# Part B of a two-part attention kernel: PSUM copies assigned to ScalarE or VectorE by place, the first K turn ahead of Q's and in two banks, and the output row in another tile's memory

## The chip, the cores and the metric

The kernel runs on one core of a Trainium2 chip. The metric is the device time in microseconds (us) of one execution. The kernel before takes 1997.98 us (median of three runs, 1996.13 to 2001.91).

## The reference

Two attention layers read their own inputs, and their outputs are laid side by side. Part A is a sliding, dilated attention; nothing in it changes here. Part B is a recurrent attention with a memory:

```python
H, Dh = 32, 192; M, seg = 8, 32          # x: (1, 2048, 640)
mem = mem0                               # 8 tokens
for s in range(64):
    xs = x[:, 32*s:32*s+32]
    h = concat([mem, xs])                # 40 tokens
    q, k, v = h @ Wq, h @ Wk, h @ Wv     # 640 -> 32 heads x 192, each
    p = softmax(mask(q @ k.T * Dh**-0.5))
    o = (p @ v) @ Wo                     # 6144 -> 640
    mem = o[:, :8]                       # the next segment needs it
    outs.append(o[:, 8:])
```

The 64 segments of 32 tokens follow one another: the first 8 rows of a segment's output are the memory of the next.

## The kernel before

Part A runs first (some 180 us) and loads part B's weights as it goes. Part B is the loop over 64 calls of `segment(s)`.

**Tiling.** The 32 heads are four groups `g` of eight. `HX` holds the tokens of a segment, turned, in two halves: `main(s)` is the 8 memory tokens and 24 tokens of x, and `ahead(s)` holds the last 8 tokens of x of four segments, which don't depend on the memory and so can be projected in advance, for several segments at once. `project32` (L440) projects 32 tokens for one group of q, k or v: 20 matmuls (5 chunks of the 640 inputs by 4 column tiles) into one PSUM tile `acc`. Each segment projects `main` for all of q, k and v; the `ahead` half is projected again only where `RENEW` says (for K of group r and V of group r+2 in a segment with s mod 4 = r), and for Q of one group at the end of each segment. A renewed projection has 40 matmuls in place of 20.

**Path of Q and K.** `to_sb` (L453) copies `acc` to SBUF (`sb`). `turn` (L458) turns it with three matmuls against the identity, into one PSUM tile `pt` (tag `x`, four buffers). `fill` (L467) copies `pt` to where the scores read it: one copy for Q (`QT`), three for K (`KT`: the outer chunks, and the middle chunk's two halves). `turn_late` (L476) does the same for the `ahead` half and keeps the rows of later segments in `Lb` tiles, from which GpSimd fills `QT` and `KT` when their segment comes.

**Scores, softmax, output.** `scores(g)` (L511) is 16 matmuls. `softmax` (L522) is six instructions on the tile `t1`, which has one buffer: L524, L528, L529 on VectorE, the exponential L530 on ScalarE, L532 and L533 on VectorE. `put_p` (L536) multiplies into `P`. `turn_p` (L545) turns `P` and copies it to `PT`; `mix` (L560) multiplies with V (`Vst`, `LV`) and copies into `OT`, four copies; `project_out` (L574) multiplies `OT` with Wo and adds up over all groups in the PSUM tile `Y`. At the end `Y` is copied to `row`, which is a tile of the tag `t1`; `memory_rows` (L586) turns its first 8 tokens into the next `HX`, and GpSimd's queue sends the other 32 to HBM (L655).

**Who copies.** Nearly all copies out of PSUM go through one function, and so appear under its line, L428:

```python
def evacuate(dst, src):
    copies["n"] += 1
    (nc.scalar.copy if copies["n"] % 2 else nc.vector.tensor_copy)(dst, src)
```

So a copy's engine depends on how many copies came before it.

**Order.** The order of TensorE's work is the order of the code in `segment` (`manual_schedule` for PE). The order on VectorE, ScalarE and GpSimd is the scheduler's. Each engine runs its instructions in order, and waits on the others where data or a buffer asks for it. An instruction that waits holds up all that stands behind it on its engine.

**Weights.** A part of Wq, Wk, Wv and Wo stays in SBUF. The rest (10 units of Wo, 8 of Wk, 6 of Wv, 320 or 384 KB each) is streamed from HBM in every segment through six buffers (`get_unit`, L394), issued from SyncE's queue as a buffer comes free.

Of the kernel before, what the change touches and what calls it, by code (L numbers as in the profile page):

```python
# [7 lines left out]
FP32 = mybir.dt.float32  # L8
BF16 = mybir.dt.bfloat16
# [255 lines left out]
def next_start(m, g, s):  # L265

    for t in range(s + 1, s + 5):
        if (m == "q" and t % 4 == g) or f"{m}{g}" in RENEW[t % 4]:
            return t


def part_b(ctx, tc, B_x, B_mem0, B_Wq, B_Wk, B_Wv, B_Wo, out, ident, n_seg, pre, nbuf, mid):
    nc = tc.nc
    Dm, H, Dh, M, SEG, L = 640, 32, 192, 8, 32, 40
# [92 lines left out]
    def pool(name, **kw):  # L367
        return ctx.enter_context(tc.tile_pool(name=name, reuse_waits="tile", **kw))
# [37 lines left out]
    QT = cpool.tile([128, 12 * L + PADW], BF16, name="QT")  # L406
    KT = cpool.tile([128, 4, 4, L], BF16, name="KT")
# [3 lines left out]
    OT = cpool.tile([128, 12 * L + PADW], BF16, name="OT")  # L411
    free = [cpool.tile([128, 3, 4, M], BF16, name=f"Lb{i}") for i in range(BLOCKS)]
    late = {}
    VW = 448
    LV = [cpool.tile([128, VW], BF16, name=f"Lv{g}") for g in range(GROUPS)]
    Vst = cpool.tile([128, VW], BF16, name="Vst")
# [5 lines left out]
        nc.gpsimd.memset(t[:, 192:256], 0.0)  # L422

    copies = {"n": 0}

    def evacuate(dst, src):
        copies["n"] += 1
        (nc.scalar.copy if copies["n"] % 2 else nc.vector.tensor_copy)(dst, src)  # L428

    def load_x(s):  # L430
        if s < n_seg:
            nc.sync.dma_start_transpose(HXs[s % 2][:], XW[s])

    def main(s):
        return HXs[s % 2][:, :, 0:SEG]

    def ahead(s):
        return HXs[s % 2][:, :, SEG:2 * SEG]

    def project32(Xs, m, g, dcs=range(5), ps=None):  # L440

        if ps is None:
            ps = [ps_acc.tile([128, 384], FP32, tag="acc", name=f"acc{n}") for n in range(len(Xs))]
        for dc in dcs:
            w = get_unit((m, g, dc))
            for n, X in enumerate(Xs):
                for j in range(4):
                    nc.tensor.matmul(ps[n][32 * j:32 * j + 32, :], lhsT=X[:, dc, :],  # L448
                                     rhs=w[:, 384 * j:384 * j + 384],
                                     start=(dc == 0), stop=(dc == 4), tile_position=(0, 32 * j))  # L450
        return ps

    def to_sb(p):  # L453
        sb = qk_sb.tile([128, 384], BF16, tag="sb", name="sb")
        evacuate(sb[:], p[:])
        return sb

    def turn(sb):  # L458
        pt = ps_x.tile([128, 3, 4, 32], FP32, tag="x")
        for c in range(3):  # L460
            nc.tensor.matmul(pt[:, c], lhsT=sb[:, 128 * c:128 * c + 128], rhs=ident, start=True, stop=True)  # L461
        return pt

    def tokens(t):
        return t[:, 0:12 * L].rearrange("p (j c n) -> p j c n", c=3, n=L)

    def fill(copy, m, n0, n1, src):  # L467

        if m == "q":
            copy(tokens(QT)[:, :, :, n0:n1].rearrange("p j c n -> p c j n"), src)  # L470
            return
        copy(KT[:, :, 0:3:2, n0:n1].rearrange("p j c n -> p c j n"), src[:, 0:3:2])
        copy(KT[0:64, :, 1, n0:n1], src[0:64, 1])
        copy(KT[64:128, :, 3, n0:n1], src[64:128, 1])  # L474

    def turn_late(sb, m, g, s, start):  # L476

        pt = turn(sb)
        for t in range(start, next_start(m, g, start)):
            rows = pt[:, :, :, M * (t % 4):M * (t % 4) + M]  # L480
            if t == s:
                fill(evacuate, m, 32, L, rows)
            else:
                late[m, g, t] = free.pop(0)
                evacuate(late[m, g, t][:], rows)

    def project_qk(s, m, g):
        renew = s == 0 or f"{m}{g}" in RENEW[s % 4]
        Xs = [ahead(s), main(s)] if renew else [main(s)]
        sbs = [to_sb(p) for p in project32(Xs, m, g)]  # L490

        def turns():
            if renew:
                turn_late(sbs[0], m, g, s, s)
            else:
                b = late.pop((m, g, s))
                fill(nc.gpsimd.tensor_copy, m, 32, L, b[:])
                free.append(b)
            fill(evacuate, m, 0, 32, turn(sbs[-1])[:])

        return turns

    def values(s, g):
        renew = s == 0 or f"v{g}" in RENEW[s % 4]
        ps = project32([ahead(s), main(s)] if renew else [main(s)], "v", g)
        for t, p in ((LV[g], ps[0]), (Vst, ps[-1]))[0 if renew else 1:]:
            v = t[:].rearrange("p (n e) -> p n e", e=64)
            w = bass.AP(v.tensor, v.offset, [v.ap[0], [256, 2], [1, 192]])
            evacuate(w, p[:].rearrange("p (h e) -> p h e", h=2))

    def scores(g):  # L511
        Sps = ps_x.tile([128, 4, L], FP32, tag="x")
# [29 lines left out]
            nc.vector.tensor_tensor(out=P[:, k, :, at:at + hi - lo], in0=t1[:, :, lo:hi],  # L542
                                    in1=sm[:].unsqueeze(2).to_broadcast([128, 4, hi - lo]), op=ALU.mult)

    def turn_p(split=1):  # L545

        pt = ps_x.tile([128, 2, 128], FP32 if split > 1 else BF16, tag="x")
        for late in range(2):
            src = P[:, late].rearrange("p a n -> p (a n)")
            if split == 1:  # L550
                nc.tensor.transpose(pt[:, late, :], src, ident)
                continue
            for h in range(2):
                nc.tensor.matmul(pt[64 * h:64 * h + 64, late, :], lhsT=src[:, 64 * h:64 * h + 64], rhs=ident,
                                 start=True, stop=True, tile_position=(0, 64 * h))
        PT = one.tile([128, 2, 2, L], BF16, tag="PT")
        evacuate(PT[:], pt[:].rearrange("p l (h n) -> p l h n", h=2)[:, :, :, 0:L])
        return PT

    def mix(g, PT):  # L560
# [37 lines left out]
    def segment(s):  # L598
        last = s + 1 == n_seg
        load_x(s + 1)  # L600
        tq, tk, PT = {}, {}, {}
        tq[0] = project_qk(s, "q", 0)
        tk[0] = project_qk(s, "k", 0)
        tq[1] = project_qk(s, "q", 1)
        tq[0]()
        tk[0]()
        tk[1] = project_qk(s, "k", 1)
        put_p(s, 0, *softmax(scores(0)))
        tq[1]()
        tk[1]()  # L610
        tq[2] = project_qk(s, "q", 2)
        values(s, 0)
        soft = softmax(scores(1))
        tq[2]()
        PT[0] = turn_p()
        put_p(s, 1, *soft)
        tk[2] = project_qk(s, "k", 2)
        mix(0, PT[0])
        values(s, 1)
        tk[2]()  # L620
        PT[1] = turn_p()
# [7 lines left out]
        tq[3]()  # L629
        tk[3]()  # L630
        PT[2] = turn_p()
# [6 lines left out]
        PT[3] = turn_p(2)  # L638
        project_out(Y, 2, range(4, 6))
        mix(3, PT[3])  # L640
        if not last:
            gl = (s + 1) % 4
            ql = project32([ahead(s + 1)], "q", gl, range(0, 3))
        project_out(Y, 3)
        row = one.tile([128, 4, L], FP32, tag="t1")
        Ysb = row[:].rearrange("p a n -> p (a n)").bitcast(BF16)
        nc.scalar.copy(Ysb, Y[:])
        if not last:
            project32([ahead(s + 1)], "q", gl, range(3, 5), ql)
            sb = qk_sb.tile([128, 384], BF16, tag="sb", name="sb")  # L650
# [82 lines left out]
```

## Time and profile before

| | |
|---|---|
| median of three runs | 1997.98 us |
| the profiled execution | 2006.95 us |
| its span, first to last instruction | 2005.2 us |
| mean granted TensorE clock | 0.992 |
| busy: PE, VectorE (DVE), ScalarE (ACT), GpSimd (POOL) | 1896.5, 1184.5, 794.9, 259.0 us |
| read from and written to HBM | 602.01 MB, 19.27 MB: 310 GB/s over the span |
| copies of `Y` to `row` (one a segment), mean distance | 28.2 us |

How to read it. Times in a timeline are us from the start of the span. "PE" rows are matmuls, "PEld" rows the loads of their stationary operand, "SPq" and "POOLq" are queues that issue DMAs. In square brackets stands how long the engine was idle before an instruction, and what ended that. L428 stands for every alternating copy, so groups are told apart by the tiles they write: `KT<-pt` is a K fill, `QT<-pt` a Q fill, `sb<-acc` a projection's copy. PE counts as busy while matmuls overlap in its pipeline; a stall shorter than 0.15 us carries no bracket and must be read from the distance of starts. A busy PE is therefore not a PE at its peak rate.

### The profile page before, as it was taken

How to read it: one execution, taken by the hardware profiler on the slowest of the kernel's cores; microseconds unless marked ns; L12 is line 12 of the kernel's file. 1: busy time of each engine (PE TensorE's matmuls, PEld its weight loads, DVE VectorE, ACT ScalarE, POOL GpSimd, SP SyncE). 2: the span in 40 equal slices, each digit the busy share in tenths (PEclk: the TensorE clock that was granted, in tenths of full speed). 3: DMA queues.
4: the chain of work that ended last, by engine and by line, in shares of the span. 5: the costliest groups of instructions: out<-in, count | busy, mean ns of one | idle time of the engine just before them, and what ended most of it. 6: DMA issues, size and time to landing. Idle time of an engine off the chain costs nothing.

```text
span 2005.2 us, 98676 instructions
## 1 busy us (share of the span) xinstructions
PE 1896.5 (95%) x42640; PEld 1211.5 (60%) x42640; DVE 1184.5 (59%) x3914; ACT 794.9 (40%) x2480; POOL 259.0 (13%) x1058
## 2 busy tenths in 40 slices
PE   7998999999999999999999999999999999999998
PEld 3655666566666666556566665666666665666665
DVE  4876565556655566556655565556655565566555
ACT  3544344333434334333433343333434333334433
POOL 2000111111111111111111111111111111111111
PEclk9999999999999999999999999999999999999999
DMA  9926999999999999999999999999999899999998
GB/s 344 316 64 239 332 332 324 323 319 319 322 312 329 327 308 333 305 304 313 322 319 319 318 324 317 331 308 317 329 319 316 301 316 303 307 308 328 322 330 277
DMA packets 279350, 621.55 MB, mean 310 GB/s; under 512 B 62089, under 2 KB 73865, under 8 KB 278601
## 3 DMA queue, kind: packets, MB, share of 16 engines
q1 hardware_dynamic: 273986, 611.14, 91.0%
q8 instruction: 334, 5.47, 1.2%
q0 software_dynamic: 4928, 4.11, 0.6%
q14 instruction: 102, 0.84, 0.1%
HBM read 602.01 MB, written 19.27 MB: 310 GB/s over the span
## 4 chain that ended last, share of the span: by engine, by line
PE 60%; DMA 16%; DVE 15%; issue 4%; ACT 4%; POOL 1%; SPq 0%; DVEq 0%; ACTq 0%; POOLq 0%
PE acc L448 24%; PE Y L582 18%; DMA out_dram<-row 7%; PE pt L461 4%; PE pq L95 3%; DMA t<-wcopy_o 3%; DMA t<-wcopy_k 3%; PE OTps L568 3%; PE Sps L517 3%; DVE sb L428 2%; DMA t<-wcopy_v 2%; DVE t L524 2%; DVE P L542 2%; PE po L161 1%; DVE mx L528 1%
## 5 line engine op out<-in xcount | busy, mean ns | idle before, releaser
L448 PEld LDWEIGHTS <-HX 128*32 128x32 bf16 x19380 | 464.9, 96 | 280.2 <-issue 52.8
L582 PEld LDWEIGHTS <-OT 128*64 128x64 bf16 x6144 | 318.1, 110 | 128.2 <-ACT OT L428 38.8
L448 PE MATMUL acc<-t,HX 128*32 128x384 bf16 x4524 | 346.1, 328 | 10.5 <-DMA t<-wcopy_k 4.2
L448 PE MATMUL acc<-wres_q,HX 128*32 128x384 bf16 x6460 | 333.8, 328 | 1.7 <-issue 1.2
L582 PE MATMUL Y<-wres_o,OT 128*64 128x320 bf16 x3584 | 332.6, 303 | 2.9 <-ACT OT L428 0.3
L582 PE MATMUL Y<-t,OT 128*64 128x320 bf16 x2560 | 268.5, 302 | 8.6 <-DMA t<-wcopy_o 6.8
L448 PE MATMUL acc<-wres_v,HX 128*32 128x384 bf16 x4520 | 254.3, 328 | 5.1 <-issue 4.0
L448 PE MATMUL acc<-wres_k,HX 128*32 128x384 bf16 x3876 | 225.0, 327 | 0.8 <-issue 0.5
L530 ACT ACTIVATE t<-t 128x160 f32<-128x160 f32 x256 | 86.2, 337 | 342.3 <-DVE t L529 340.4
L428 DVE CAST sb<-acc 128x384 bf16<-128x384 f32 x291 | 160.8, 553 | 92.2 <-PE acc L448 75.6
L461 PE MATMUL pt<-ident,sb 128*128 128x128 bf16 x1938 | 179.6, 222 | 14.7 <-DVE sb L428 4.8
L428 ACT CAST sb<-acc 128x384 bf16<-128x384 f32 x292 | 138.8, 475 | 129.9 <-PE acc L448 125.7
L428 ACT CAST KT<-pt 64x128 bf16<-64x128 f32 (+3 forms) x517 | 139.3, 277 | 127.6 <-DVE KT L428 86.7
L461 PEld LDWEIGHTS <-sb 128*128 128x128 bf16 x1938 | 110.6, 97 | 90.0 <-issue 37.2
L524 DVE SCALAR_TENSOR_TENSOR t<-Sps,mask 128x160 f32<-128x160 f32 x256 | 82.8, 323 | 138.3 <-PE Sps L517 103.1
L428 ACT CAST OT<-OTps 128x120 bf16<-128x120 f32 x512 | 106.9, 261 | 126.5 <-PE OTps L568 124.9
L428 DVE CAST KT<-pt 64x128 bf16<-64x128 f32 (+2 forms) x452 | 134.1, 300 | 31.2 <-ACT KT L428 21.9
L428 DVE CAST OT<-OTps 128x120 bf16<-128x120 f32 x512 | 125.0, 270 | 45.5 <-PE OTps L568 45.2
L474 POOL COPY KT<-Lb 64x32 bf16<-64x32 bf16 x189 | 40.7, 215 | 825.0 <-PE Sps L517 820.4
L517 PEld LDWEIGHTS <-QT 128*64 128x64 bf16 x4096 | 101.6, 112 | 70.2 <-issue 59.2
L428 ACT CAST Vst<-acc 128x384 bf16<-128x384 f32 x205 | 98.6, 481 | 98.8 <-PE acc L448 95.3
L517 PE MATMUL Sps<-KT,QT 128*64 128x40 bf16 x4096 | 120.9, 187 | 16.1 <-DVE KT L428 11.3
(84 smaller groups left out, 1959.9 us busy)
## 6 DMA issues: line engine op xcount, KB each, us to landing
t<-wcopy_o SPq DMA_DIRECT2D x640, 320.0 KB, 4.7
t<-wcopy_k SPq DMA_DIRECT2D x512, 384.0 KB, 5.3
t<-wcopy_v SPq DMA_DIRECT2D x384, 384.0 KB, 5.4
wres_q<-in_B_Wq_dram SPq DMA_DIRECT2D x20, 384.0 KB, 7.6
wres_v<-in_B_Wv_dram SPq DMA_DIRECT2D x14, 384.0 KB, 7.4
wres_k<-in_B_Wk_dram SPq DMA_DIRECT2D x12, 384.0 KB, 6.4
wres_o<-in_B_Wo_dram SPq DMA_DIRECT2D x14, 320.0 KB, 7.5
wcopy_o<-in_B_Wo_dram SPq DMA_DIRECT2D x10, 320.0 KB, 7.5
```

Of the source, the lines that this page charges most:

```text
L95: nc.tensor.matmul(pq[32 * d:32 * d + 32], lhsT=wcol[:, k, t, 4 * c + d, :], rhs=xTs[s][:, k, :], start=(k == 0), stop=(k == 4), tile_posi ...
L161: nc.tensor.matmul(po[:, c % 2, :], lhsT=ident, rhs=prod[:, w, :], start=(w == 0), stop=(w == W - 1))
L428: (nc.scalar.copy if copies["n"] % 2 else nc.vector.tensor_copy)(dst, src)
L448: nc.tensor.matmul(ps[n][32 * j:32 * j + 32, :], lhsT=X[:, dc, :], rhs=w[:, 384 * j:384 * j + 384], start=(dc == 0), stop=(dc == 4), tile_ ...
L461: nc.tensor.matmul(pt[:, c], lhsT=sb[:, 128 * c:128 * c + 128], rhs=ident, start=True, stop=True)
L474: copy(KT[64:128, :, 3, n0:n1], src[64:128, 1])
L517: nc.tensor.matmul(Sps[64 * g2:64 * g2 + 64, a, :], lhsT=QT[:, at:at + 64], rhs=KT[:, a, ((0, 1), (3, 2))[g2][part], :], start=(n == 0), s ...
L524: nc.vector.scalar_tensor_tensor(out=t1[:], in0=Sps[:], scalar=scale, in1=mask[:].unsqueeze(1).to_broadcast([128, 4, L]), op0=ALU.mult, op ...
L530: nc.scalar.activation(t1[:], t1[:], ACTF.Exp)
L542: nc.vector.tensor_tensor(out=P[:, k, :, at:at + hi - lo], in0=t1[:, :, lo:hi], in1=sm[:].unsqueeze(2).to_broadcast([128, 4, hi - lo]), op ...
L568: nc.tensor.matmul(ps[a][:, k, :], lhsT=V[32 * a:32 * a + 32, col:col + 128], rhs=PT[32 * a:32 * a + 32, late, half, :], start=(n == 0), s ...
L582: nc.tensor.matmul(Y[64 * gv:64 * gv + 64, :], lhsT=OT[:, L * c:L * c + 64], rhs=w[:, n:n + 320], start=(i == 0 and r == 0), stop=(i == 23 ...
```

## The change

The copies' engines are written into tables (`ENGINES`), by kind of copy and group; only the copies of `OT` and of the `Lb` tiles still alternate. K's fills go to ScalarE alone, except that of group 0. For group 0, K is turned ahead of Q, its middle chunk first and into a PSUM tile of its own, which VectorE copies, while ScalarE copies the outer chunks from another tile. `project_qk` hands back two functions (turn the `ahead` half, turn `main`) in place of one; `both` calls the two. `Y`'s copy goes to the first 320 columns of `OT` in place of a `t1` tile.

```diff
+    S_, V_ = nc.scalar.copy, nc.vector.tensor_copy
+    ENGINES = {"sb": {"q": (V_, S_, S_, S_), "k": (S_, S_, S_, S_)}, "late": (V_, V_, V_, V_),
+               "QT": (V_, S_, S_, V_), "KT": (S_, S_, S_, S_), "V": (S_, V_, V_, S_), "LV": (V_, S_, S_, V_),
+               "PT": (S_, V_, V_, V_)}
...
-    def to_sb(p):
+    def to_sb(p, copy):
         sb = qk_sb.tile([128, 384], BF16, tag="sb", name="sb")
-        evacuate(sb[:], p[:])
+        copy(sb[:], p[:])
...
-    def turn(sb):
-        pt = ps_x.tile([128, 3, 4, 32], FP32, tag="x")
-        for c in range(3):
-            nc.tensor.matmul(pt[:, c], lhsT=sb[:, 128 * c:128 * c + 128], rhs=ident, start=True, stop=True)
+    def turn(sb, chunks=(0, 1, 2)):
+        pt = ps_x.tile([128, len(chunks), 4, 32], FP32, tag="x", name="pt")
+        for k, c in enumerate(chunks):
+            nc.tensor.matmul(pt[:, k], lhsT=sb[:, 128 * c:128 * c + 128], rhs=ident, start=True, stop=True)
...
-        copy(KT[:, :, 0:3:2, n0:n1].rearrange("p j c n -> p c j n"), src[:, 0:3:2])
-        copy(KT[0:64, :, 1, n0:n1], src[0:64, 1])
-        copy(KT[64:128, :, 3, n0:n1], src[64:128, 1])
+        fill_outer(copy, n0, n1, src[:, 0:3:2])
+        fill_middle(copy, n0, n1, src[:, 1])
...
             if t == s:
-                fill(evacuate, m, 32, L, rows)
+                fill(S_, m, 32, L, rows)
...
-            fill(evacuate, m, 0, 32, turn(sbs[-1])[:])
+        def turn_main():
+            if m == "k" and g == 0:
+                fill_middle(V_, 0, 32, turn(sbs[-1], (1,))[:, 0])
+                fill_outer(S_, 0, 32, turn(sbs[-1], (0, 2))[:])
+            else:
+                fill(ENGINES["QT" if m == "q" else "KT"][g], m, 0, 32, turn(sbs[-1])[:])
...
-        tq[0]()
-        tk[0]()
+        tq[0][0]()
+        both(tk[0])
+        tq[0][1]()
...
-        row = one.tile([128, 4, L], FP32, tag="t1")
-        Ysb = row[:].rearrange("p a n -> p (a n)").bitcast(BF16)
+        Ysb = OT[:, 0:320]
         nc.scalar.copy(Ysb, Y[:])
```

The copies of V and of `PT` take their engine from the same tables (`values`, `turn_p`); all other calls of a turn become `both(...)`, at the same places. The number and shapes of the instructions stay as they were; 451 copies move from VectorE to ScalarE over the whole program, net.

More of the change, by code (lines that the diff above doesn't have):

```diff
@@ L424, in part_b @@
     copies = {"n": 0}
+    S_, V_ = nc.scalar.copy, nc.vector.tensor_copy
+    ENGINES = {"sb": {"q": (V_, S_, S_, S_), "k": (S_, S_, S_, S_)}, "late": (V_, V_, V_, V_),
+               "QT": (V_, S_, S_, V_), "KT": (S_, S_, S_, S_), "V": (S_, V_, V_, S_), "LV": (V_, S_, S_, V_),
+               "PT": (S_, V_, V_, V_)}
     def evacuate(dst, src):
         copies["n"] += 1
-        (nc.scalar.copy if copies["n"] % 2 else nc.vector.tensor_copy)(dst, src)
+        (S_ if copies["n"] % 2 else V_)(dst, src)
     def load_x(s):
@@ L471, in fill, with fill_outer, fill_middle @@
             return
-        copy(KT[:, :, 0:3:2, n0:n1].rearrange("p j c n -> p c j n"), src[:, 0:3:2])
-        copy(KT[0:64, :, 1, n0:n1], src[0:64, 1])
-        copy(KT[64:128, :, 3, n0:n1], src[64:128, 1])
+        fill_outer(copy, n0, n1, src[:, 0:3:2])
+        fill_middle(copy, n0, n1, src[:, 1])
+    def fill_outer(copy, n0, n1, src):
+        copy(KT[:, :, 0:3:2, n0:n1].rearrange("p j c n -> p c j n"), src)
+    def fill_middle(copy, n0, n1, src):
+        copy(KT[0:64, :, 1, n0:n1], src[0:64])
+        copy(KT[64:128, :, 3, n0:n1], src[64:128])
     def turn_late(sb, m, g, s, start):
@@ L489, in project_qk, with turn_ahead @@
         Xs = [ahead(s), main(s)] if renew else [main(s)]
-        sbs = [to_sb(p) for p in project32(Xs, m, g)]
-        def turns():
+        ps = project32(Xs, m, g)
+        sbs = [to_sb(p, c) for p, c in zip(ps, [ENGINES["late"][g], ENGINES["sb"][m][g]][2 - len(ps):])]
+        def turn_ahead():
             if renew:
@@ L498, in turns, with both @@
                 free.append(b)
-            fill(evacuate, m, 0, 32, turn(sbs[-1])[:])
-        return turns
+        def turn_main():
[4 more added lines that the diff above has]
+                fill(ENGINES["QT" if m == "q" else "KT"][g], m, 0, 32, turn(sbs[-1])[:])
+        return turn_ahead, turn_main
+    def both(turns):
+        for t in turns:
+            t()
     def values(s, g):
@@ L505, in values @@
         ps = project32([ahead(s), main(s)] if renew else [main(s)], "v", g)
-        for t, p in ((LV[g], ps[0]), (Vst, ps[-1]))[0 if renew else 1:]:
+        for t, p, copy in ((LV[g], ps[0], ENGINES["LV"][g]), (Vst, ps[-1], ENGINES["V"][g]))[0 if renew else 1:]:
             v = t[:].rearrange("p (n e) -> p n e", e=64)
             w = bass.AP(v.tensor, v.offset, [v.ap[0], [256, 2], [1, 192]])
-            evacuate(w, p[:].rearrange("p (h e) -> p h e", h=2))
+            copy(w, p[:].rearrange("p (h e) -> p h e", h=2))
     def scores(g):
@@ L543, in put_p, with turn_p @@
                                     in1=sm[:].unsqueeze(2).to_broadcast([128, 4, hi - lo]), op=ALU.mult)
-    def turn_p(split=1):
+    def turn_p(g):
+        split = 2 if g == 3 else 1
         pt = ps_x.tile([128, 2, 128], FP32 if split > 1 else BF16, tag="x")
@@ L556, in turn_p @@
         PT = one.tile([128, 2, 2, L], BF16, tag="PT")
-        evacuate(PT[:], pt[:].rearrange("p l (h n) -> p l h n", h=2)[:, :, :, 0:L])
+        ENGINES["PT"][g](PT[:], pt[:].rearrange("p l (h n) -> p l h n", h=2)[:, :, :, 0:L])
         return PT
@@ L604, in segment @@
         tq[1] = project_qk(s, "q", 1)
-        tq[0]()
-        tk[0]()
+        tq[0][0]()
+        both(tk[0])
+        tq[0][1]()
         tk[1] = project_qk(s, "k", 1)
         put_p(s, 0, *softmax(scores(0)))
-        tq[1]()
-        tk[1]()
+        both(tq[1])
+        both(tk[1])
         tq[2] = project_qk(s, "q", 2)
@@ L613, in segment @@
         soft = softmax(scores(1))
-        tq[2]()
-        PT[0] = turn_p()
+        both(tq[2])
+        PT[0] = turn_p(0)
         put_p(s, 1, *soft)
@@ L619, in segment @@
         values(s, 1)
-        tk[2]()
-        PT[1] = turn_p()
+        both(tk[2])
+        PT[1] = turn_p(1)
         Y = ps_y.tile([128, 320], FP32, tag="y")
@@ L628, in segment @@
         values(s, 2)
-        tq[3]()
-        tk[3]()
-        PT[2] = turn_p()
+        both(tq[3])
+        both(tk[3])
+        PT[2] = turn_p(2)
         project_out(Y, 1, range(0, 4))
@@ L637, in segment @@
         project_out(Y, 2, range(0, 4))
-        PT[3] = turn_p(2)
+        PT[3] = turn_p(3)
         project_out(Y, 2, range(4, 6))
```

## The prediction

> **What bounds the kernel now.** I read the page's busy rows and slices first, then the windows, then the waits, and then the timeline of part B, since a share says nothing of short stalls.
>
> ```profile
> PE 1896.5 (95%) x42640; PEld 1211.5 (60%) x42640; DVE 1184.5 (59%) x3914; ACT 794.9 (40%) x2480; POOL 259.0 (13%) x1058
> ...
> DMA  9926999999999999999999999999999899999998
> ```
>
> Two resources are near their end at once: PE, and the DMA engines that stream weights. The windows (last two numbers: DMA share, GB/s) say how near:
>
> ```profile
> 200.00:300.00 100.00, 95.28 (x2236) 62.36 (x2234) 57.57 (x206) 38.24 (x126) 11.61 (x48) 0.98 0.98 332
> 300.00:700.00 400.00, 384.79 (x9051) 247.20 (x9051) 234.73 (x835) 157.40 (x513) 55.70 (x231) 1.00 0.95 322
> 700.00:1100.00 400.00, 379.98 (x8895) 242.69 (x8891) 231.02 (x826) 155.07 (x504) 53.23 (x221) 1.00 0.96 315
> ```
>
> With 1100:1500 (0.96, 321) and 1500:1900 (0.94, 313) the share is 0.9525 and the rate 318 GB/s on average, so a segment of 28.23 us moves 8.98 MB. ScalarE and VectorE are half idle; what counts is whether PE stands behind a copy of theirs. One segment (s mod 4 = 2) from its first turn to its first `turn_p`:
>
> ```profile
> 811.01 0.51 PE L461 MATMUL pt<-ident,sb 128*128 128x128 bf16 x6
> ...
> 812.28 0.26 ACT L428 CAST KT<-pt 64x128 bf16<-64x128 f32 x1 [0.35 <-DVE KT L428]
> 812.37 0.63 PE L517 MATMUL Sps<-KT,QT 128*64 128x40 bf16 x16
> ...
> 814.57 0.32 DVE L524 SCALAR_TENSOR_TENSOR t<-Sps,mask 128x160 f32<-128x160 f32 x1 [1.51 <-DMA out_dram<-row]
> ...
> 815.16 0.41 DVE L428 CAST KT<-pt 128x256 bf16<-128x256 f32 x1
> ...
> 815.61 0.26 ACT L428 CAST KT<-pt 64x128 bf16<-64x128 f32 x1 [1.82 <-DVE KT L428]
> 815.84 0.34 ACT L530 ACTIVATE t<-t 128x160 f32<-128x160 f32 x1
> 815.90 0.29 DVE L428 CAST KT<-pt 64x128 bf16<-64x128 f32 x1
> ...
> 817.14 0.40 PE L551 MATMUL pt<-ident,P 128*128 128x128 bf16 x2 [0.20 <-DVE P L542]
> ```
>
> Two faults show. K's three copies pass from engine to engine, each waiting for the last one's end, and the scores wait for the third. And the softmax stands 1.51 us behind the row's DMA, because `row` sits in the only `t1` buffer; K's next copies stand behind it on VectorE, and so the second scores and `turn_p` come late. The waits name the handovers:
>
> ```profile
> ACT KT L428 <- DVE KT L428: 86.7, 176, 3.1
> DVE KT L428 <- ACT KT L428: 21.9, 63, 0.7
> DVE t L524 <- DMA out_dram<-row: 19.9, 18, 3.0
> ```
>
> PE's stalls are mostly too short for that list. I measure them from starts on the timeline, first turn to second `turn_p`, against the least time of each piece in any segment (6 turns 0.44 us, 9 0.61; 20 projection matmuls 0.93, 40 1.74, 60 2.55; scores 0.36; 3 turns 0.18, `turn_p` 0.21, `mix` 0.30). Medians for s mod 4 = 0, 1, 2, 3 are 8.39, 8.90, 9.57, 9.40 us; the pieces add up to 7.16, 8.02, 8.78, 7.80. The stall is 1.23, 0.88, 0.79, 1.60, on average 1.13 us a segment; all pieces of a whole segment add up to 26.1, so of the 2.1 us over that some 1.0 lie elsewhere, mostly in projections and output products that read streamed tiles.
>
> **The change, part by part.**
>
> *Row in `OT`.* L524 no longer waits for the DMA. In its place the first `OT` copies of the next segment's group 0 wait for it, one on ScalarE (K's copies of group 2 and an exponential behind it) and one on VectorE (`Vst`, `PT` behind it). From the copy of `Y` they stand 0.6 + 0.5 + 0.3 + 2.6 us (rest of the segment's end, next projections) and 6.6 us (first turn to end of `mix`) away, 10.5 in all; the DMA lands 5.3 us after issue (median). Cost nothing; were that cover gone, each us late costs one. The DMA's issue stays behind the same copy on GpSimd's queue.
>
> *First K turn.* K's middle chunk starts at time 0. A copy starts 0.27 us after its turn's last matmul (811.12 to 811.38 for Q). Copies that don't wait on each other start closer than they last: two `OT` copies of 0.26 us take 0.42 on ScalarE, 0.16 apart; `sb` and `Vst`, 0.36 apart; on VectorE two of 0.27 take 0.46. So VectorE copies K's halves at 0.27 and 0.48, Q at 0.69 to 1.24; ScalarE, after `sb`, the outer chunks at 0.53 to 0.90. PE reaches the scores at 1.36: no wait, where the scores lost 0.20 us (0.56 for 0.36) with s mod 4 = 2 or 3 and 0.58 with 0. What is late next is the copy of k1's `sb`: 0.17 us in three of four.
>
> *K's fills on ScalarE, softmax free.* In the changed program's order VectorE runs the softmax of groups 0 and 1 nearly unbroken. For s mod 4 = 3: L524 follows the scores' start by 0.49, so 1.85; L528 0.36 on, L529 0.35 on, done by 2.95. On ScalarE Q's copy starts at 2.11 and K's at 2.47, 2.72, 2.87, so the exponential starts at 3.02, 0.07 late; L532 3.40, L533 0.35 on, `P` from 3.97 to 4.37. PE reaches `turn_p` at 4.62, or 4.44 without the wait for `sb`. No wait; the trace lost 0.5 there and up to 0.5 at the second scores. The next softmax starts at 4.57; its exponential stands behind `PT`'s copy until 5.67, and `P` is ready at 7.03; PE comes at 7.16. With 0 and 2 the margins are the same or wider. With 1 the late K adds four copies on ScalarE; its last K piece ends at 4.74, the scores come at 4.98.
>
> These starts rest on copies of the one engine overlapping for K too. Laid end to end at full duration, `turn_p` would wait 0.58 us with s mod 4 = 0 or 3 and the second scores 0.93 with 1; with the rest, 0.76 on average. So the remaining stall lies between 0.13 and 0.76. I take 0.2, nearest to the rows that show overlap: of 1.13 us, 0.9 saved, 64 times, 58 us.
>
> A handover of one PSUM tile between the two engines costs 0.35 us here (812.28), more than the 0.16 to 0.25 by which a copy follows another on the same engine, so I count K on ScalarE alone as a gain. The Trainium skill ("TensorEngine Tiling (Array Packing)", PSUM Bottleneck) says to use ScalarE and VectorE both for copies out of PSUM, which speaks against it. By that rule the second scores would keep their stall (0.2 us a segment on average, 13 us in all), and the sum would be 45 in place of 58 us. The trace bears it out only across tiles, not within one.
>
> *Load.* 451 copies move: at each shape's mean duration ScalarE goes from 795 to about 951 us, VectorE from 1184 to about 1008; neither becomes the bound.
>
> *What DMA leaves of it.* PE gets its weights through six buffers. PE without waits for weights now takes about 27.2 us a segment; the changed one 26.3. The DMA engines, at 318/0.9525 = 334 GB/s for a share of 1, need 26.9. So PE was the tighter limit and DMA becomes it. If DMA didn't give at all, nothing is saved; at the 0.98 that the window 200:300 shows, a segment takes 28.23 x 0.9525/0.98 = 27.44, 50 us less; PE allows 58. I take half of what PE allows, 0.45 us a segment, as the rest comes back as waits for weights: 28 us.
>
> The profiled execution took 2006.95 us (span 2005.2 and 1.75 around it), 0.45% over the median. 2006.95 - 28 = 1979; the same 28 from the median gives 1970.
>
> **The rivals.**
>
> *DMA gives way.* SyncE waits for a buffer that PE has yet to free most of the time (628.6 us for projections, 309.3 for `Y`), so DMA could start earlier. Then all 58 us come: 1940, with rest 1936 to 1953. Against it: 0.95 of the engines' time is busy. The Trainium skill ("DMA: Bandwidth & Descriptors", Specifications) gives about 358 GB/s of HBM for a core; by it a segment needs 25.1 us and this rival holds. The best long window here has 332.
>
> *DMA takes nearly all.* The segments from 807 to 896 us take 29 us and more (window 803:831: 308 GB/s at 0.95); if the stream sets the pace so throughout, 8 to 18 us remain: 1980 to 1990. Or less than 6: no change.
>
> *ScalarE's queue becomes the bound: slower.* If K's three copies on ScalarE, which share a PSUM tile, waited for each other's end, 0.2 us would come between them, and the exponential behind them would start 0.4 us later than end to end, in both early softmaxes. 0.76 + 0.33 (second `turn_p`) + 0.8 = 1.9 us of stall against 1.13: 0.76 x 64 = 49 us, half of it taken up by DMA's idle time: 2023. It turns to a loss once the exponentials start about 0.75 us late. Against it: in groups 0 and 1 the program gives the copies after the first no wait.
>
> **How the numbers follow.** A measurement here tells 0.3%, 6 us. Forecast 1970 (own range 1958 to 1980): 0.50. DMA gives way: 0.17. DMA takes nearly all, 1980 to 1991: 0.19. Within 6 us: 0.07. Slower: 0.07. So faster 0.86, same 0.07, slower 0.07. 1942 to 1991 leaves out the slower cases, no change, and the lowest third of the second case: 0.2.
>
> **What would show it.** After: no wait of the softmax's first instruction for `out_dram`; the KT handovers (108.6 us) under 10; first scores at 0.36 us in all four kinds; first turn to second `turn_p` within 0.3 us of 7.16, 8.02, 8.78 and 7.80 where no weight is late; ScalarE near 950 us; the DMA share near 0.97, and more PE idle time before matmuls on streamed tiles (10.5 and 8.6 us now). I am wrong if the exponential starts over 0.3 us after L529's end, if an `OT` copy waits for the row's DMA, or if PE's stretch shrinks by 0.9 us and the segment doesn't shrink by 0.2 to 0.7.

## The result, and the profile after

The changed kernel takes 1989.27 us (median of 20 runs, 1979.5 to 1994.75) beside 1998.42 us for the kernel before (20 runs, 1991.86 to 2008.14): a ratio of 0.9944, 95% interval 0.9928 to 0.9959. Run once more (e9 below) it came to 0.9921, interval 0.9893 to 0.9949. So it saves 9 to 16 us where the forecast said 28. The span of the profiled executions, one of each kernel, went from 2005.2 to 1988.4 us, 16.8 less.

The page of the changed kernel: busy times, and a group of PE, whose last columns are the idle time before it and what ended most of it:

```profile
PE 1878.1 (94%) x42640; PEld 1208.2 (61%) x42640; DVE 1059.3 (53%) x3463; ACT 912.0 (46%) x2931; POOL 255.4 (13%) x1058
...
L604 PE MATMUL Y<-wres_o,OT 128*64 128x320 bf16 x3584 | 331.5, 302 | 8.7 <-DVE OT L432 4.7
```

The work moved from VectorE to ScalarE, if less far than worked out (the page gives ScalarE 912 us and VectorE 1059; 951 and 1008 were the estimates). New is that output products on resident tiles, which need no weight from the stream, stand idle 8.7 us (2.9 before), over half of it for an `OT` copy on VectorE. The windows show that the stream hardly runs faster than before (0.96 and 315 GB/s in the same window):

```profile
700.00:1100.00 400.00, 381.55 (x9055) 246.83 (x9054) 209.86 (x749) 186.35 (x622) 53.89 (x229) 1.00 0.96 320
```

The waits answer two of the forecast's signs. The softmax's first instruction waits only for the scores; no wait on `out_dram` stands ahead of it or of an `OT` copy. K's copies wait for the turn, no longer for one another across engines (108.6 us before):

```profile
DVE t L545 <- PE Sps L538: 160.2, 160, 2.2
ACT KT L480 <- PE pt L465: 87.6, 110, 2.8
```

But the timeline of a segment of the kind shown of before (s mod 4 = 2; first turn at 809.32) goes another way than the forecast's:

```profile
809.32 0.51 PE L465 MATMUL pt<-ident,sb 128*128 128x128 bf16 x6
...
809.58 0.28 DVE L483 CAST KT<-pt 64x128 bf16<-64x128 f32 x1 [1.22 <-PE pt L465]
...
809.87 0.38 ACT L480 CAST KT<-pt 128x256 bf16<-128x256 f32 x1
809.88 0.29 DVE L484 CAST KT<-pt 64x128 bf16<-64x128 f32 x1
...
810.21 0.56 DVE L474 CAST QT<-pt 128x384 bf16<-128x384 f32 x1
...
810.86 0.43 PE L538 MATMUL Sps<-KT,QT 128*64 128x40 bf16 x16
811.23 0.51 PE L465 MATMUL pt<-ident,sb 128*128 128x128 bf16 x6
...
811.98 0.38 ACT L480 CAST KT<-pt 128x256 bf16<-128x256 f32 x1
...
812.08 0.36 DVE L550 TENSOR_TENSOR t<-t,mx 128x160 f32<-128x160 f32 x1
812.25 0.26 ACT L483 CAST KT<-pt 64x128 bf16<-64x128 f32 x1
...
812.52 0.26 ACT L484 CAST KT<-pt 64x128 bf16<-64x128 f32 x1
812.81 0.34 ACT L551 ACTIVATE t<-t 128x160 f32<-128x160 f32 x1
```

Read the starts of neighbours on one engine. On VectorE K's second half starts 0.30 us behind the first, Q 0.33 behind the second: each after the other's end. On ScalarE the first half starts 0.27 us behind the outer chunks, which last 0.38; but the second half starts 0.27 us behind the first, which lasts 0.26, and the exponential 0.29 us behind the second. So Q's copy starts at 0.89 us of the stretch (forecast 0.69), the scores at 1.54 (1.36), the exponential at 3.49 (3.02 with s mod 4 = 3, where 3.49 is read as well). It starts 0.37 us after the end of the softmax's third instruction (L550, before L529), one of the forecast's signs of being wrong. The scores now last 0.37 us as forecast, but only because their wait moved ahead of them: to the next turn it is 1.91 us from the first, and it was 1.92 before.

The medians of the stretch from first turn to second `turn_p`, read off the starts on the timeline, for s mod 4 = 0, 1, 2, 3:

| | 0 | 1 | 2 | 3 |
|---|---|---|---|---|
| before | 8.39 | 8.90 | 9.57 | 9.40 |
| forecast, free of stalls | 7.16 | 8.02 | 8.78 | 7.80 |
| after | 8.04 | 8.47 | 8.98 | 8.38 |
| e1, row alone | 8.43 | 8.73 | 9.18 | 8.71 |
| e7, middle on 128 partitions | 7.63 | 8.29 | 8.96 | 8.45 |

The stall in it fell from 1.13 to 0.53 us on average; the forecast took 0.2 (bounds 0.13 to 0.76).

### The profile page after: what moved, and what is told of

It is laid out like the page before. It is cut to its first block, busy times and chain, and to the rows that moved or that the text cites. A ratio compares the mean times of both kernels' runs of the same rounds, so it can differ in the third digit from the quotient of the medians.

```text
span 1988.4 us, 98934 instructions
## 1 busy us (share of the span) xinstructions
PE 1878.1 (94%) x42640; PEld 1208.2 (61%) x42640; DVE 1059.3 (53%) x3463; ACT 912.0 (46%) x2931; POOL 255.4 (13%) x1058
## 4 chain that ended last, share of the span: by engine, by line
PE 68%; DMA 16%; ACT 7%; DVE 4%; issue 3%; SPq 1%; ACTq 0%; POOL 0%; POOLq 0%; DVEq 0%
PE acc L452 33%; PE Y L604 18%; DMA t<-wcopy_k 7%; PE pt L465 6%; DMA t<-wcopy_v 4%; PE Sps L538 3%; PE OTps L590 3%; PE pq L95 2%; DMA t<-wcopy_o 2%; ACT sb L673 1%; ACT OT L669 1%; DMA wcopy_o<-in_B_Wo_dram 1%; PE pt L573 1%; ACT sb L459 1%; PE po L161 1%
## 5 line engine op out<-in xcount | busy, mean ns | idle before, releaser
L459 ACT CAST sb<-acc 128x384 bf16<-128x384 f32 x448 | 211.1, 478 | 168.8 <-PE acc L452 147.2
L604 PE MATMUL Y<-t,OT 128*64 128x320 bf16 x2560 | 264.2, 301 | 3.5 <-DMA t<-wcopy_o 2.4
L480 ACT CAST KT<-pt 128x256 bf16<-128x256 f32 (+1 forms) x323 | 110.4, 342 | 90.4 <-PE pt L465 87.6
L553 DVE TENSOR_REDUCE sm<-t 128x4 f32<-128x160 f32 x256 | 81.9, 320 | 128.9 <-ACT t L551 128.9
L484 POOL COPY KT<-Lb 64x32 bf16<-64x32 bf16 x189 | 40.2, 213 | 806.1 <-PE Sps L538 673.0
L538 PE MATMUL Sps<-KT,QT 128*64 128x40 bf16 x4096 | 113.6, 187 | 7.9 <-ACT KT L480 2.4
L618 DVE CAST HX<-pt 128x40 bf16<-128x40 f32 x63 | 12.6, 199 | 177.8 <-PE pt L615 177.8
L563 DVE TENSOR_TENSOR P<-t,sm 128x128 bf16<-128x128 f32 (+1 forms) x512 | 100.0, 236 | 11.3
```

The source lines that it names most:

```text
L459: copy(sb[:], p[:])
L538: nc.tensor.matmul(Sps[64 * g2:64 * g2 + 64, a, :], lhsT=QT[:, at:at + 64], rhs=KT[:, a, ((0, 1), (3, 2))[g2][part], :], start=(n == 0), s ...
L553: nc.vector.tensor_reduce(out=sm[:], in_=t1[:], axis=AX.X, op=ALU.add)
L604: nc.tensor.matmul(Y[64 * gv:64 * gv + 64, :], lhsT=OT[:, L * c:L * c + 64], rhs=w[:, n:n + 320], start=(i == 0 and r == 0), stop=(i == 23 ...
```

## The experiments

Ratios are against the kernel before on the same chip.

**e1: the row alone**, on the kernel of before.

```diff
-        row = one.tile([128, 4, L], FP32, tag="t1")
-        Ysb = row[:].rearrange("p a n -> p (a n)").bitcast(BF16)
+        Ysb = OT[:, 0:320]
```

> The kernel before, with one part of the change alone: Y's copy goes to OT in place of a t1 tile. If the row's wait was the main fault of before (1.5 us on VectorE ahead of the first softmax of a segment), this alone gives most of the gain of the whole change: 8 to 15 us less than before (ratio 0.992 to 0.996), and the stalls at the second scores and the first turn_p (12.6 and 16.7 us in the trace of before) fall by more than half. If the gain came from the engine tables, it gives under 4 us (0.998 or more).

1984.17 us, ratio 0.9911 (0.9884 to 0.9937): some 17 us, more than the 8 to 15 expected and no less than the whole change. In the table above the row alone takes 0.17 to 0.69 us from the stretch in three kinds; the second scores, which lost 0.25 and 0.51 us with s mod 4 = 1 and 3, stand at 0.36 to 0.38.

**e2: the change without the row** (the same three lines the other way round, on the changed kernel).

> The changed kernel with the row back in a t1 tile: tables and K's first turn alone. If the row is what counts, the time is within 4 us of before or above it (0.998 to 1.004), as K's copies on ScalarE now stand behind nothing but the exponential still waits. If the tables count, it keeps 6 us or more (0.997 or less).

1994.4 us, ratio 0.9973 (0.9957 to 0.9989): some 5 us, between the two expectations. So with the stream the tables and the first K turn do save a little where the row still waits.

**e3, e4: before and after without the stream**: resident units of the same width in place of the streamed ones.

```diff
-        t = wstream.tile([128, SLOT], BF16, tag="ws")
-        nc.sync.dma_start(t[:, 0:unit_cols(u)], copied[u])
-        return t[:, 0:unit_cols(u)]
+        return next(res[r] for r in res if r not in wait and unit_cols(r) == unit_cols(u))
```

> The kernel before with no weights streamed in part B: each streamed unit is replaced by a resident unit of the same width, so the streamed weights' part of the result is left out, and PE's instructions stay as they are. It gives PE's time with the copies' stalls alone. From the trace of before, waits on streamed tiles are 0.54 us a segment: about 1998 - 35 = 1963 us, ratio 0.982; if the waits that I could not assign are weights too (0.75 us a segment), 1950.

> The changed kernel with the same replacement of streamed units. Theory 1 (the copies' stalls fell far less than I forecast, 0.3 to 0.4 us a segment, and weights take back little): 19 to 25 us less than the kernel before without streaming. Theory 2 (the forecast saving of 0.9 us a segment is there and waits for weights take it back): 45 to 58 us less.

1930.55 and 1920.9 us: 0.965 (0.9627 to 0.9672) and 0.9601 (0.9579 to 0.9624). e3 lies below both values expected of it (1963 and 1950): the row's wait, some 17 us by e1, went as well. Without a stream to wait for, the change saves 9.7 us, less than either theory's, and not 58. So it isn't that PE saved 58 us and the weights took them: PE's side was far smaller than forecast. In e3 the row's DMA lands before the softmax asks for `t1` (second scores at 0.36 to 0.38 us there too), so these 9.7 us are the tables and the first K turn alone.

**e8: e1 without the stream** (e1's and e3's diffs together).

> The kernel of before with the row in OT's memory alone, and with streamed units replaced by resident ones of the same width, as in e3 and e4 (other weights, so another result). Theory 1 (without the stream the row's DMA lands early, so moving the row is worth nothing, and what the tables and the first K turn save stands alone): within 2 us of e3's 1930.6, so tables and first K turn are worth 8 to 10 us where no weight is waited for. Theory 2 (moving the row saves more than that wait): 1915 to 1922, as e4 or below it, and tables and first K turn are worth nothing even there.

1932.02 us, 0.9651 (0.9628 to 0.9674): like e3. So moving the row is worth nothing where its DMA lands early, and the tables and first K turn are worth 11.1 us on top of it (e4). By kind, medians of all pieces of a whole segment:

| | 0 | 1 | 2 | 3 |
|---|---|---|---|---|
| e8 | 27.73 | 27.08 | 26.99 | 26.56 |
| e4 | 27.21 | 26.67 | 26.56 | 27.21 |

They gain 0.41 to 0.52 us in three kinds and lose 0.65 in the fourth: mean 0.175, times 64 = 11 us. The 0.65 has three places: 0.13 in the stretch, 0.26 at the last scores, and 0.27 from v3's projection to the end of the output products behind it. The timeline of the changed kernel shows the last two (s mod 4 = 3):

```profile
853.46 0.21 ACT L480 CAST KT<-pt 128x64 bf16<-128x64 f32 x1 [0.86 <-PE pt L465]
...
854.09 0.38 ACT L480 CAST KT<-pt 128x256 bf16<-128x256 f32 x1
...
854.64 0.26 ACT L484 CAST KT<-pt 64x128 bf16<-64x128 f32 x1
854.69 0.67 PE L538 MATMUL Sps<-KT,QT 128*64 128x40 bf16 x16
...
856.90 0.32 DVE L553 TENSOR_REDUCE sm<-t 128x4 f32<-128x160 f32 x1 [0.46 <-ACT t L551]
...
857.13 0.27 DVE L432 CAST OT<-OTps 128x120 bf16<-128x120 f32 x1
...
857.46 0.46 PE L604 MATMUL Y<-wres_o,OT 128*64 128x320 bf16 x4 [0.31 <-DVE OT L432]
```

The late K's three copies (the first is shown) now stand on ScalarE too, ahead of K's own, and the scores take 0.67 us in place of 0.41. And `OT`'s first copy still goes by alternation; with the other copies out of the count, its turn falls on VectorE in this kind, behind a sum that waits for the exponential (the releaser of 857.46).

**e5: the first K turn undone**, tables and row kept.

```diff
-            if m == "k" and g == 0:
-                fill_middle(V_, 0, 32, turn(sbs[-1], (1,))[:, 0])
-                fill_outer(S_, 0, 32, turn(sbs[-1], (0, 2))[:])
-            else:
-                fill(ENGINES["QT" if m == "q" else "KT"][g], m, 0, 32, turn(sbs[-1])[:])
+            fill(ENGINES["QT" if m == "q" else "KT"][g], m, 0, 32, turn(sbs[-1])[:])
...
-        tq[0][0]()
+        both(tq[0])
         both(tk[0])
-        tq[0][1]()
```

> The changed kernel with its first K turn undone: K is turned behind Q again, into one bank, and all of its copies go to ScalarE; the tables and the row in OT's memory stay. Theory 1 (the first K turn is a gain, though a smaller one than forecast, and the loss lies later in the segment): the first scores wait some 0.2 us in all four kinds, the ratio rises from 0.9944 to about 0.997. Theory 2 (the first K turn is what spoils the gain that the row alone brings, 0.991): the ratio falls to about 0.991.

1987.45 us, 0.9932 (0.9908 to 0.9956): between the theories, and not apart from the changed kernel. The stretch is 8.26, 8.47, 8.91, 8.12: the K turn gains 0.22 us with s mod 4 = 0 and loses 0.07 with 2 and, by the least times of the kind (8.04 without it, 8.19 with it), 0.15 with 3. In these two kinds the second turn comes 1.75 us after the first without it and 1.91 with it.

**e6: the two places of s mod 4 = 3 mended**, on the changed kernel.

```diff
-                fill(S_, m, 32, L, rows)
+                fill(V_ if g == 3 and m == "k" else S_, m, 32, L, rows)
...
-            evacuate(OT[:, 3 * L * a:3 * L * a + 3 * L], ps[a][:].rearrange("p k n -> p (k n)"))
+            (S_ if a % 2 == 0 else V_)(OT[:, 3 * L * a:3 * L * a + 3 * L], ps[a][:].rearrange("p k n -> p (k n)"))
```

> The changed kernel with two assignments altered: OT's four copies go by place (ScalarE, VectorE, ScalarE, VectorE in every kind, where the changed kernel still alternates and puts the first on VectorE with s mod 4 = 3), and the late K of group 3 goes to VectorE in place of ScalarE. Theory 1 (the tables give back in groups 2 and 3 what they save in groups 0 and 1): the scores of group 3 lose their 0.25 us and the output products of group 2 their 0.4 us with s mod 4 = 3; some 15 us of stall in all (5 before the scores, 10 before the products) go down to under 5, and the time falls by 6 to 10 us, to a ratio of 0.990 to 0.991. Theory 2 (weights take back whatever copies save): the stalls go and the ratio stays at 0.994.

1979.72 us, 0.9887 (0.9861 to 0.9913), clear of the first measurement of the changed kernel; its interval overlaps e9's a little. The scores are back at 0.41 us, and the output products start 0.92 us after v3's projection (1.31 in the changed kernel), with no wait:

```profile
965.52 0.41 PE L538 MATMUL Sps<-KT,QT 128*64 128x40 bf16 x16
...
966.72 0.51 PE L452 MATMUL acc<-wres_v,HX 128*32 128x384 bf16 x8
...
967.34 0.40 ACT L594 CAST OT<-OTps 128x120 bf16<-128x120 f32 x2
...
967.64 0.46 PE L604 MATMUL Y<-wres_o,OT 128*64 128x320 bf16 x4
```

**e7: K's middle copies on 128 partitions**, at the same length.

```diff
-        copy(KT[0:64, :, 1, n0:n1], src[0:64])
-        copy(KT[64:128, :, 3, n0:n1], src[64:128])
+        copy(KT[:, :, 1, n0:n1], src)
+        copy(KT[:, :, 3, n0:n1], src)
```

> The changed kernel with K's two middle copies on all 128 partitions each, with the same columns and so the same length (what should stay zero is overwritten, so another result is computed). Theory 1 (a copy on 64 partitions does not overlap with the copy behind it on its engine, one on 128 does): each middle copy's successor starts 0.14 to 0.21 us behind its start in place of 0.28; Q's first copy starts at 0.6 to 0.7 us of the segment's first turn in place of 0.89, the scores at 1.36 in place of 1.55, the first exponential near 3.02 in place of 3.49, and the time falls by 5 to 15 us. Theory 2 (copies that read one PSUM tile follow each other at full length, whatever their partitions): nothing moves, the ratio stays within 0.002 of 0.9944.

1975.36 us, 0.9863 (0.983 to 0.9896). The copies last as long as before and now start closer (s mod 4 = 2, first turn at 916.73):

```profile
917.00 0.29 DVE L483 CAST KT<-pt 128x128 bf16<-128x128 f32 x1 [1.21 <-PE pt L465]
...
917.20 0.28 DVE L484 CAST KT<-pt 128x128 bf16<-128x128 f32 x1
...
917.40 0.55 DVE L474 CAST QT<-pt 128x384 bf16<-128x384 f32 x1
...
918.09 0.43 PE L538 MATMUL Sps<-KT,QT 128*64 128x40 bf16 x16
...
919.50 0.27 ACT L483 CAST KT<-pt 128x128 bf16<-128x128 f32 x1
919.66 0.28 ACT L484 CAST KT<-pt 128x128 bf16<-128x128 f32 x1
919.82 0.36 ACT L551 ACTIVATE t<-t 128x160 f32<-128x160 f32 x1
```

0.20 us apart on VectorE and 0.16 on ScalarE where it was 0.30 and 0.27; Q at 0.67, the scores at 1.36, the exponential at 3.09. These are close to the forecast's starts (0.69, 1.36, 3.02). Only the partitions changed, so they decide. The last scores of s mod 4 = 3 are back at 0.25 us to the next group here too (0.51 in the changed kernel), with the late K still on ScalarE.

It isn't the number of partitions, though. In the trace of before, VectorE copies K's first half (partitions 0 to 63; the second half, on ScalarE, waits for it) with a copy on 128 partitions behind it:

```profile
323.21 0.28 DVE L428 CAST KT<-pt 64x128 bf16<-64x128 f32 x1
323.42 0.22 DVE L428 COPY PT<-pt 128x160 bf16<-128x160 bf16 x1
...
323.53 0.26 ACT L428 CAST KT<-pt 64x128 bf16<-64x128 f32 x1 [0.35 <-DVE KT L428]
```

The copy of `PT` starts 0.21 us behind a copy of 0.28: it overlaps as on 128 partitions in e7. The late K's first half, 0.17 us long, has `PT` 0.10 us behind it in that trace. In e6 the same `PT` stands behind the second half (partitions 64 to 127, L484), 0.22 us:

```profile
853.54 0.19 DVE L484 CAST KT<-pt 64x32 bf16<-64x32 f32 x1
853.76 0.24 DVE L579 COPY PT<-pt 128x160 bf16<-128x160 bf16 x1
```

So 64 partitions overlap where they are the first ones; what doesn't is the second half, with the copy ahead of it and with the one behind. Whether the change of the first partition does it or the upper half itself, no run tells apart.

**e9, e10: the changed kernel and the row alone once more, side by side.**

> The changed kernel once more, beside e10 and e11 on one chip. Theory 1 (what the row alone brings is as much as the whole change: the tables and the first K turn give back in groups 2 and 3, at the first turns and in waits for weights what they save): a ratio of 0.993 to 0.995, within 0.003 of e10's. Theory 2 (the tables and the first K turn cost time on top of the row): 0.0035 or more over e10's.

> The kernel of before with the row in OT's memory alone, once more beside the changed kernel on one chip. Theory 1: 0.991 to 0.994, the same as e9 within the intervals. Theory 2: 0.989 to 0.991, clear of e9.

1984.11 us, 0.9921 (0.9893 to 0.9949), and 1982.15 us, 0.9913 (0.9887 to 0.994): the same. With the stream, and with the row moved, the tables and the first K turn are worth nothing that these runs can tell (5 us where the row isn't moved, e2), beside 11 us without it.

**e11: e6 with masked middle copies**: 128 partitions, times a column that is 1 on 64 partitions and 0 on the others.

```diff
+        for h, k in ((0, 1), (1, 3)):
+            dst, m = KT[:, :, k, n0:n1], half[:, h:h + 1]
+            if copy is S_:
+                nc.scalar.activation(dst, src, ACTF.Copy, scale=m)
+            elif copy is V_:
+                nc.vector.tensor_scalar_mul(dst, src, m)
```

> e6 (OT's copies by place, late K of group 3 on VectorE) with K's two middle copies, on ScalarE and VectorE, written on all 128 partitions as a product with a column that is 1 on 64 partitions and 0 on the others; the reference's result is computed. Theory 1 (a copy on 64 partitions keeps its engine from starting the next one early, and that is what the forecast missed): first scores at 1.36 us with s mod 4 = 2 and 3, first exponential near 3.1, and a time below both e6 and e7: e6 saved 0.0057 on the changed kernel's ratio, e7 0.0081, together 0.9806, less what weights take back: 0.979 to 0.986. Theory 2 (weights set the floor that e6 and e7 reached): 0.986 to 0.989.

1972.9 us, 0.987 (0.984 to 0.9901): 26 us under the kernel before by that ratio, 29 by the medians, and 11 under the changed one (e9), on the same chip. The ratio is theory 2's, and its interval reaches into theory 1's. It doesn't tell the theories apart: a masked copy costs more (0.34 to 0.35 us on VectorE and 0.38 on ScalarE, for 0.28 and 0.26), so the scores start at 1.44 and not at 1.36, though the copies do overlap (0.26 to 0.27 us apart on VectorE).

**e12: the middle chunk copied once**, the zeros left out, the scores' matmuls of that chunk on 64 rows.

```diff
+        copy(KT[:, :, 1, n0:n1], src)
...
+                chunk = g2 + part
+                r0, r1 = (64 * g2, 64 * g2 + 64) if chunk == 1 else (0, 128)
-                nc.tensor.matmul(Sps[64 * g2:64 * g2 + 64, a, :], lhsT=QT[:, at:at + 64],
+                nc.tensor.matmul(Sps[64 * g2:64 * g2 + 64, a, :], lhsT=QT[r0:r1, at:at + 64],
```

> e6 with K's middle chunk copied once, on all 128 partitions, and the zeros left out: the scores' matmuls of that chunk take only the 64 rows of their head, of QT and of KT. One copy of three is gone from every K fill, GpSimd's too, and no copy on 64 partitions is left; the reference's result is computed. Theory 1 (the 64-partition copies are what the forecast missed, and the stream leaves part of what goes with them): first scores at 1.36 us with s mod 4 = 2 and 3 and at 1.53 with 0, no wait of the second turn_p for P, first exponential before 3.0 us; a ratio of 0.978 to 0.985, below e6 and e7. Theory 2 (the stream sets a floor near 0.987, which e6, e7 and e11 reached): the stalls go, waits for streamed tiles grow by as much, 0.986 to 0.989.

2119.57 us, 1.0596 (1.0564 to 1.0627): both theories missed. The stalls went (the scores' group has no idle time before it), but the scores themselves went from 0.36 to 1.24 us, 0.88 x 4 x 64 = 225 us at most. The page of e12:

```profile
L539 PE MATMUL Sps<-KT,QT 128*64 128x40 bf16 (+1 forms) x4096 | 332.2, 204 | 0.0
```

**e13: e12 with the eight matmuls on 128 rows first, then the eight on 64.**

```diff
-            a, part = n // 2, n % 2
+            a, middle = n % 4, n // 4
...
-                chunk = g2 + part
+                chunk = 1 if middle else 2 * g2
```

> e12 with the order of the scores' matmuls changed: first the eight on 128 rows, then the eight on 64. Theory 1 (PE pays some 55 ns at each change between 128 and 64 rows, 0.88 us over e12's 16 matmuls; with one change in and one out it is about 0.1): scores at 0.4 to 0.5 us in place of 1.24; and the gains of e6 and e7 add: a ratio of 0.976 to 0.984. Theory 2 (a floor near 0.987 set by the stream): scores as in theory 1, waits for streamed tiles grow, 0.986 to 0.989. Theory 3 (a matmul on 64 rows is itself that much slower): scores at 0.9 us or more, a ratio over 1.02.

1977.49 us, 0.9896 (0.987 to 0.9923): the scores as theories 1 and 2 have them, the ratio over both. The same matmuls in another order take 0.47 us, 0.105 over their least time before in groups 0 to 2, and 0.44 for 0.25 in group 3: 32 us in all, which eats much of what the missing copies save.

**e14: e6 and e7 together** (both diffs above).

> e6 and e7 in one: OT's copies by place, late K of group 3 on VectorE, K's two middle copies on 128 partitions each (what should stay zero is overwritten, so another result is computed). Theory 1 (the gains add: e6 0.0057 and e7 0.0081 below 0.9944, or 0.0034 and 0.0058 below e9's 0.9921): 0.979 to 0.984. Theory 2 (floor set by the stream): 0.986 to 0.989.

1970.17 us, 0.9861 (0.9828 to 0.9894): theory 2's ratio; the two gains did not add measurably, and one of them, at the last scores of s mod 4 = 3, is in both. Its profile is less plain: the pieces' medians sum to 26.72 us a segment, against 26.99 in e6 and 26.84 in e7, and the mean segment is 27.64 us against 27.83 and 27.70. Nor does the stream stand at a ceiling; it moves 321 to 329 GB/s in the four long windows at a share of 0.96, more than after's 318 to 323. Whether a floor lies near 0.986 stays open.

**e15: e13 without the stream.**

> e13 with streamed units replaced by resident ones of the same width, as in e3, e4 and e8 (other weights, so another result). Theory 1 (the rest of the forecast saving on the side of PE is there to be had once no copy is on 64 partitions and groups 2 and 3 are mended): e4's 1920.9 less 62 times 0.2 to 0.4 us, 1896 to 1909. Theory 2 (the copies were worth no more than e4 showed): 1915 to 1921.

1917.9 us, 0.9588 (0.9565 to 0.9611), by its number theory 2's. But the expectation left out the 32 us that e13's scores cost on PE. With them taken off, e15 would stand near 1886, 35 us under e4: that is worked out, not run.

## Why the prediction was right and wrong

The sum said 0.9 us a segment on PE's side; the pieces of the profiled executions fell by 0.40. Of the 0.5 that are missing, 0.33 lie in the stretch and 0.13 behind it.

**The row: right, and most of the gain.** The wait is gone, and the `OT` copies that took its place never wait for the DMA. Alone it gives 0.991, as much as the whole change. The forecast credited a part of the same stall to K's handovers, for which the second scores were its example. e8 shows otherwise: with the row's wait gone and K's copies still passing between engines, the second scores take 0.36 to 0.38 us in all kinds. The Trainium skill ("TensorEngine Tiling (Array Packing)", PSUM Bottleneck) advises to use both engines for copies out of PSUM; by the forecast's reading of it the sum would have been 45. The runs don't bear that reading out: with K's copies, late ones too, on ScalarE alone, the second scores of s mod 4 = 1 go from 0.38 to 0.66 us (e8 to e4), but with the same copies on ScalarE and on 128 partitions they take 0.36 (e7).

**First K turn: the step that failed.** "VectorE copies K's halves at 0.27 and 0.48, Q at 0.69" took the spacing from copies that all lie on 128 partitions and put it on K's two halves, which the kernel before never had behind each other on one engine. The second half follows the first, and Q the second half, end to end (0.30, 0.33). The scores' 0.20 us became a wait ahead of them, and only s mod 4 = 0 gained (0.35 us to the next turn). The handover that this was to save was misread too: 0.35 us at 812.28 is how long ScalarE stood idle. From start to start the two halves are 0.31 us apart there (811.97 to 812.28), hardly more than the 0.27 to 0.30 on one engine. That K1's `sb` would be late next was right: where the scores come at 1.36 (e7), the turn of K1 waits 0.18 us for it.

**K on ScalarE: the same error, twice as long.** The exponential came at 3.49 for 3.02: 0.19 from the late scores, 0.28 from the halves. With the row alone moved and K's copies passing between the engines (e1, e8) it comes at 3.34 to 3.35 at the least in these kinds (s mod 4 = 2 and 3), so here the tables and the first K turn made it later. The forecast named this ("rest on copies of the one engine overlapping for K too") and bounded the stall at 0.76; it took 0.2 for the likeliest value, and 0.53 was measured: 0.33 x 64 = 21 us. At each kind's least time e7 has 0.20 of these 0.33 back.

**Groups 2 and 3: not costed at all.** The tables and the alternation that stays were weighed in the first stretch only. In s mod 4 = 3 they lose 0.53 us behind it, 16 x 0.53 = 8.5 us (e4, e6); the half of it at the last scores goes with the second halves, too (e7).

**What weights take back: about right, of much less.** The pieces' medians fell from 27.49 to 27.09 us a segment, 26 us in all, where the sum said 58. The mean segment fell from 28.24 to 27.98, 16.5 us, which is the span's difference. So 0.36 of the smaller gain was lost to late weights and other scattered waits in these two executions, and by the 9 to 16 us of all runs between 0.4 and 0.65, where the forecast took half. PE's idle time before streamed tiles went from 10.5 and 8.6 us to

```profile
L452 PE MATMUL acc<-t,HX 128*32 128x384 bf16 x4524 | 345.3, 328 | 21.1 <-DMA t<-wcopy_k 8.8
...
L604 PE MATMUL Y<-t,OT 128*64 128x320 bf16 x2560 | 264.2, 301 | 3.5 <-DMA t<-wcopy_o 2.4
```

5.5 us more in sum. The expected share of 0.97 didn't come (0.95 to 0.96). The rival by which DMA takes nearly all gave the measured time (1980 to 1991), but e4 speaks against its reason: without the stream there was no 58 us either. That tables and first K turn are worth 11 us without the stream (e8, e4) and, on top of the row, nothing measurable with it (e9, e10) is shown; how the stream undoes them piece by piece is not.

**Slower by ScalarE's queue: right in kind.** The end-to-end copies of that rival are what came, for the second half alone; its further 0.2 us between copies, and so its loss, did not.

## What to carry to other kernels

Before you price a chain of short copies by how closely others follow each other, find rows in which the copy and both its neighbours lie on the same partitions as yours: the same length, and even the same number of partitions, were not enough here. When a kernel's copies leave a common alternation, look at every copy that stays in it, in each kind of loop pass: its engine changes too. A wait that ends inside a group can move ahead of it and leave the group's own time as forecast: measure from one fixed start to the next.

## What the runs showed of the hardware

- On VectorE a copy out of PSUM on partitions 0 to 63 let the next instruction start before its end: 0.20 to 0.21 us behind its start, for 0.27 to 0.28 (before), as on 128 partitions (0.20 to 0.21 for 0.28 to 0.29, e7). A copy on partitions 64 to 127 neither overlapped with the one on 0 to 63 ahead of it (0.30 us apart) nor let the one on 128 partitions behind it overlap (0.33 for 0.29).
- ScalarE did the same with the second half: 0.27 to 0.29 us from start to start on either side of it, for 0.26. On 128 partitions with the same columns it was 0.16 for 0.27 to 0.28 (e7).
- Matmuls on 128 and on 64 rows by turns cost far more than their work: 16 matmuls with eight changes took 1.24 us, the same 16 with one change in and one out 0.47, and all on 128 rows 0.36 (groups 0 and 1). The Trainium skill ("TensorEngine Tiling (Array Packing)", Key Properties) says that changing the tiling mode drains TensorE; these runs agree in that each change costs time, 0.88/8 = 0.11 us in e12.
- A segment's row, written out by DMA, held up the next softmax only while weights streamed: from issue to landing it took 5.3 us (median) beside the stream and 1.7 without it, where the wait was gone with nothing moved (e3).
